# Recurrent-memory attention: the softmax of heads 16 to 31 moved ahead of the queries of heads 0 to 15, and the last tokens projected for sixteen segments at a time

## The chip, the cores and the metric

The kernel runs on one core of a Trainium2 chip (trn2). The time is device time in microseconds (us) of one execution of the whole program, and the median over runs is compared. A profiled execution of the same kernel gives the trace from which all durations below are taken.

## The reference, cut to what matters

The input x has 2048 tokens of width 640 in bf16. Four layers run one after the other, A, B, A, B, each on the layer norm of x and each added to x. Both A layers are the same linear-memory attention and are not touched. A B layer is a segmented attention with a recurrent memory of 8 tokens:

```python
for s in range(n_seg):                       # 64 segments of 32 tokens
    h = concatenate([mem, xs])               # 8 + 32 = 40 tokens
    q, k, v = h @ Wq, h @ Wk, h @ Wv         # 32 heads of width 128
    p = softmax(where(mask, q @ k.T * scale, -1e9))
    o = (p @ v) @ Wo                         # back to width 640
    mem = o[:8]                              # the next segment's memory
    outs.append(o[8:])                       # 32 rows of output
```

The rows of `o` are shifted by 8 against the tokens: the memory that a segment hands on comes from its first 8 rows. So segment s+1 can't be projected before segment s is finished, and the whole B layer is a chain of 64 steps.

## The kernel before

All weights of a B layer lie in SBUF. A step works on 32 columns (`cols_of`): 8 columns of memory that the last step made and 24 columns of the next segment. Projecting those takes the weights as the moving operand: `thin_mm` runs 20 matmuls of 512 columns, four at a time in four strips of 32 columns of the array, and gives the projection of 16 heads for the 32 tokens. There are six such blocks in a step: Ka, Qa, Kb, Qb (keys and queries, a for heads 0 to 15, b for heads 16 to 31) and, later, Va and Vb. The remaining 8 tokens of each segment, here called its last tokens, don't depend on the chain. They are projected ahead of time and kept in DRAM (`QKd` for queries and keys, `VTd` for values), from where every step loads its own share.

The step in its written order, which is also the order of every compute engine's queue (each instruction of TensorE, ScalarE, VectorE and GpSimd is tied to the one written before it on that engine; only the DMA queue of SyncE is ordered by the scheduler):

- The four blocks Ka, Qa, Kb, Qb; each is copied to SBUF (`kq`), transposed (`transp4`, tiles TPak, TPaq, TPbk, TPbq) and scattered into the head-wise tiles `KT` and `QT`: the 8 memory columns by VectorE for this step, the 24 others by ScalarE for the next.
- `mask_mm` writes the mask into the two score tiles in PSUM: SP0 with groups 0 to 7 (the last tokens of all heads, and heads 0 to 15), SP1 with groups 8 to 11 (heads 16 to 31). `scores` adds the products.
- The softmax: `soft_max`, `soft_sub` and `soft_sum` on VectorE, `soft_exp` on ScalarE, then the reciprocal and the products `Px` on VectorE and `Pm` on GpSimd. Meanwhile TensorE does Va, Vb and the first 30 matmuls of `tail_unit`.
- `p_transp` (PTP) transposes the probabilities, `pv` (OTP) multiplies them by the values, `o_mm` (OPS, and OPSd for the deferred rows, `od_chunk`) multiplies by Wo.
- The 8 new memory rows go from OPS by ScalarE (`msb`) to TensorE (MT, which transposes them) and by VectorE (`b_HX`) into the columns of the next step. Between the parts of MT lie the matmuls of `vtail_unit`.

The work on last tokens is cut into units, one for each step. A batch T holds 8 segments, 64 tokens (`TX[T]`), and has eight units. `tail_unit` has 40 matmuls with a 128x128 piece of Wq or Wk as the stationary operand and 64 moving columns; `vtail_unit` has 20 matmuls of 256 moving columns in strips of 32. Steps without a unit of their own repeat one as filler (`work`). A layer norm is made for 128 tokens (`ln_norm`, then `ln_spread`, five transposes), and its result is shared out: 24 tokens of each segment to `HX`, 8 to `TX`.

PSUM is a ring of five shared buffers (`ps_tile`) besides a few of their own (`po`): a tile must be read out before the fifth tile after it can be written.

Of the kernel before, what the change touches and what calls it, by code (L numbers as in the profile page):

```python
# [29 lines left out]
NCH = 5  # L30
# [568 lines left out]
def layer_B(nc, tc, C, W, x_src, xb_src, x_dst, mem0, B_Wv, B_Wo, nsteps=64, out_bf16=False, tag=""):  # L599
# [4 lines left out]
    NT = nsteps // 8  # L604
    QKd = tc.dram_tile([nsteps, 128, 512], BF16, name=f"b_QKd{tag}")
    VTd = tc.dram_tile([nsteps, 8, 4096], BF16, name=f"b_VTd{tag}")
    with ExitStack() as ctx:
# [4 lines left out]
        hp = pool("b_hx", 4)  # L612
# [73 lines left out]
        def ln_load(g, home=None):  # L686
            pool_, tg = home or (bx, "xt")
            xt = pool_.tile([128, D], BF16, name="b_xt", tag=tg)
            nc.sync.dma_start(xt[:], xb_src[128 * g:128 * g + 128, :])
            ln_xt[g] = xt  # L690

        def ln_norm(g):
            xt = ln_xt[g]
            layernorm_tile(nc, sml, C, xt[:], xt[:], "b_ln")
            ln_ready.append(g)

        def ln_spread(g):
            xt = ln_xt.pop(g)
            tps = ps_tile([128, NCH, 4, 32], BF16, "b_lntps")
            for c in range(NCH):  # L700
                nc.tensor.transpose(tps[:, c, :, :].rearrange("p i t -> p (i t)"), xt[:, 128 * c:128 * c + 128], C.identb[:])
            HX[g] = hp.tile([128, NCH, 4, 32], BF16, name="b_HX", tag="HX")
            T, half = divmod(g, 2)
            if half == 0:
                TX[T] = tx.tile([128, NCH, 8, 8], BF16, name="b_TX", tag="TX")
            nc.scalar.copy(HX[g][:, :, :, 8:32], tps[:, :, :, 0:24])
            nc.scalar.copy(TX[T][:, :, 4 * half:4 * half + 4, :], tps[:, :, :, 24:32])
# [6 lines left out]
        def thin_mm(cols_ap, Wt, b, name):  # L714
            ps = ps_tile([128, 512], F32, name)
            for c in range(NCH):
# [38 lines left out]
        tail_ps = {}  # L755

        def tail_unit(T, k, i0, i1, shared=False):
            proj, hg = divmod(k, 4)
            Wt = W.wk if proj else W.wq
            if i0 == 0:  # L760
                if shared:
                    tail_ps[0] = ps_tile([128, 8, 64], F32, "b_tail")
                else:
                    tail_ps[0] = po.tile([128, 8, 64], F32, name="b_tail", tag="tail")
            ps = tail_ps[0]
            for i in range(i0, i1):
                h = 8 * hg + i
                for c in range(NCH):
                    nc.tensor.matmul(ps[:, i, :], lhsT=Wt[:, c, 128 * h:128 * h + 128], rhs=TX[T][:, c, :, :].rearrange("p s t -> p (s t)"),
                                     start=(c == 0), stop=(c == NCH - 1))  # L770

        def tail_evac(T, k, eng, home=None):
            proj, hg = divmod(k, 4)
            pool_, tg = home or (wk, "tu")
            tu = pool_.tile([128, 8, 8, 8], BF16, name="b_tu", tag=tg)
            evac(eng, tu[:].rearrange("p s h t -> p h s t"), tail_ps[0][:].rearrange("p h (s t) -> p h s t", t=8),
                 None if proj else SCB)
            o = 256 * proj + 64 * hg
            nc.sync.dma_start(QKd[8 * T:8 * T + 8, :, o:o + 64].rearrange("s p f -> p s f"), tu[:].rearrange("p s h t -> p s (h t)"))

        def vtail_unit(T, k, c0=0, c1=NCH, ps=None):
            b4, ch = divmod(k, 2)
            if ps is None:
                ps = ps_tile([128, 256], F32, "b_vtail")
            for c in range(c0, c1):
                for q in range(4):
# [6 lines left out]
        def vtail_evac(T, k, ps, eng, home="vt"):  # L793
            b4, ch = divmod(k, 2)
            vt = wk.tile([128, 256], BF16, name="b_vt", tag=home)
            evac(eng, vt[:], ps[:])
            for jj in range(2):
                o = 512 * (2 * b4 + jj) + 256 * ch
                nc.sync.dma_start(VTd[8 * T:8 * T + 8, :, o:o + 256].rearrange("s t f -> (s t) f"), vt[64 * jj:64 * jj + 64, :])
# [17 lines left out]
        n0 = min(4, NG)  # L817
        for g in range(n0):
            ln_load(g, homes[g])
        load_B_wv(nc, W, B_Wv)  # L820
        for g in range(min(2, n0)):
            ln_norm(g)
# [5 lines left out]
        for k in range(8):  # L828
            tail_unit(0, k, 0, 8, shared=True)
            tail_evac(0, k, "act" if k % 2 == 0 else "dve", (kqp, "kq"))  # L830
            if k % 4 == 1 and 2 + k // 4 < n0:
                ln_norm(2 + k // 4)
            if k % 4 == 3 and 2 + k // 4 < n0:
# [24 lines left out]
        if NT > 1:  # L858
            tail_unit(1, 0, 0, 8, shared=True)
            tail_evac(1, 0, "act")  # L860
            vtail_evac(1, 0, vtail_unit(1, 0), "dve")
# [46 lines left out]
        def ln_g(s):  # L908
            return 2 * (s // 8) + 4 + (s % 8 == 5)

        def ln_xt_due(s):
            return s % 8 in (2, 5) and ln_g(s) < NG

        for s in range(nsteps):
# [3 lines left out]
            unit = None  # L918
            if (s + 1) // 8 + 1 < NT:
                unit = ((s + 1) // 8 + 1, (s + 1) % 8)  # L920
            work = unit or (None if last else (NT - 1, 0))
# [24 lines left out]
            def scores(SPs):  # L946
                for b in range(2):
                    for j in range(4):
                        for i in range(4):
                            h = 16 * b + 4 * j + i  # L950
                            nc.tensor.matmul(SPs[b][32 * i:32 * i + 32, j + 4 * (1 - b), :], lhsT=QT[s][:, h, :], rhs=KT[s][:, h, :],
                                             start=False, stop=True, tile_position=(0, 32 * i), skip_group_check=True)
                    if b == 0:
                        qz = QZ[s % 2][:].rearrange("p x c -> p (x c)")
                        for j in range(4):
                            for e in range(2):
                                for t4 in range(4):
                                    pr = 8 * (t4 // 2) + 2 * j + t4 % 2
                                    nc.tensor.matmul(SPs[0][32 * t4:32 * t4 + 16, j, :], lhsT=qz[:, 24 * pr + 8 * e:24 * pr + 8 * e + 16],
                                                     rhs=KT[s][:, 2 * pr + e, :],  # L960
                                                     start=False, stop=True, tile_position=(0, 32 * t4), skip_group_check=True)
# [6 lines left out]
            def soft_max(a, SP):  # L968
                nc.vector.tensor_reduce(out=negmax[:, slice(*GR[a])], in_=SP[:], axis=AX.X, op=ALU.max, negate=True)

            def soft_sub(a, SP):
                n_ = GR[a][1] - GR[a][0]
                nc.vector.tensor_tensor(out=SP[:], in0=SP[:], in1=negmax[:, slice(*GR[a])].unsqueeze(2).to_broadcast([128, n_, 40]), op=ALU.add)

            def soft_exp(a, SP):
                nc.scalar.activation(out=E_[:, slice(*GR[a]), :], in_=SP[:], func=ACT.Exp)

            def soft_sum(a):
                nc.vector.tensor_reduce(out=ssum[:, slice(*GR[a])], in_=E_[:, slice(*GR[a]), :], axis=AX.X, op=ALU.add)
# [24 lines left out]

            Ka = thin_mm(cols, W.wk, 0, "b_Ka")
            ka = kq(Ka, "act")
            Qa = thin_mm(cols, W.wq, 0, "b_Qa")
            qa = kq(Qa, "dve", SCB)
            Kb = thin_mm(cols, W.wk, 1, "b_Kb")
            kb = kq(Kb, "act")  # L1010
            Qb = thin_mm(cols, W.wq, 1, "b_Qb")
            qb = kq(Qb, "act", SCB)

            TPak = transp4(ka, "b_TPak")
            scatter("dve", TPak, 0, KT[s], 0, 8, 32)
            x_scatter(TPak, 0, KT)
# [3 lines left out]
            TPbk = transp4(kb, "b_TPbk")  # L1020
            scatter("dve", TPbk, 1, KT[s], 0, 8, 32)
            x_scatter(TPbk, 1, KT)
            SPa = mask_mm(0)
            TPbq = transp4(qb, "b_TPbq", po.tile([128, 4, 128], BF16, name="b_TPbq", tag="tail"))
            scatter("dve", TPbq, 1, QT[s], 0, 8, 24)
            x_scatter(TPbq, 1, QT)
            SPb = mask_mm(1)
            scores((SPa, SPb))
            soft_max(0, SPa)
            soft_max(1, SPb)  # L1030
            soft_sub(0, SPa)
            soft_exp(0, SPa)
            soft_sub(1, SPb)
            soft_exp(1, SPb)
            soft_sum(0)
            soft_sum(1)
# [14 lines left out]
            if work:  # L1051
                tail_unit(work[0], work[1], 0, 6)
# [7 lines left out]
            if work:  # L1060
                tail_unit(work[0], work[1], 6, 8)
            if unit:
                tail_evac(unit[0], unit[1], "act")
# [22 lines left out]
            if ln_xt_due(s):  # L1086
                ln_norm(ln_g(s))
# [25 lines left out]
            vtail_some(NCH)  # L1113
            if unit:
# [113 lines left out]
```

## Time and profile before

| | |
|---|---|
| median of 3 runs | 2796.26 us (2792.15 to 2801.13) |
| profiled execution | 2787.25 us, its span 2785.5 us |
| TensorE busy | 2574.7 us (92%), 65414 matmuls |
| VectorE / ScalarE / GpSimd busy | 61% / 57% / 26% |
| first B layer: first Ka of step 0 to first Ka of step 63 | 432.6 to 1379.3 us |
| second B layer, the same | 1819.2 to 2764.0 us |

These two stretches of 63 steps are 1892 us of the span. The time of a matmul in the profile is its latency: matmuls overlap, so what a block of them costs is read from the start of one block to the start of the next. A form such as 128*32 says how many rows and columns of the array a matmul uses.

### The profile page before, as it was taken

What the parts mean: (1) busy time and instruction counts of PE and PEld (TensorE: products, weight loads), DVE (VectorE), ACT (ScalarE), POOL (GpSimd) and SP (SyncE); (2) the same over time, 40 slices, a digit from 0 to 9 for tenths busy, and PEclk for the clock granted to TensorE, in tenths of its full rate; (3) what the DMA queues carried; (4) which work ended last, traced back from release to release, by engine and by line L of the source; (5) the groups of instructions that cost most, each with busy time, mean ns of one, the idle gap of its engine ahead of it and who ended that gap; (6) DMA issues with size and microseconds to landing.
All of it is one profiled execution on the core that took longest, in us unless ns stands there. A gap on an engine that the chain in (4) does not pass through costs nothing. (4 is left out here: it accounts for less than half of the span.)

```text
span 2785.5 us, 146956 instructions
## 1 busy us (share of the span) xinstructions
PE 2574.7 (92%) x65414; PEld 1700.1 (61%) x65480; DVE 1686.6 (61%) x4553; ACT 1584.9 (57%) x3708; POOL 715.2 (26%) x1645
## 2 busy tenths in 40 slices
PE   5888879999999999999978888799999999999998
PEld 3555556666666666666645555556666666666665
DVE  6888854555555555555578888445555555555554
ACT  4888854555555555544458888445555455555443
POOL 4666541111111111111146665411111111111110
PEclk9999979999999999999989999899999999999999
DMA  6111162221212212111120111721211121211110
GB/s 239 41 44 40 30 195 69 45 46 41 45 43 45 43 43 45 43 39 30 41 99 28 51 49 37 231 47 39 42 42 40 40 44 40 43 41 38 39 26 20
DMA packets 322300, 156.36 MB, mean 56 GB/s; under 512 B 245760, under 2 KB 310400, under 8 KB 318592
## 3 DMA queue, kind: packets, MB, share of 16 engines
q1 hardware_dynamic: 320224, 136.47, 19.2%
q8 instruction: 512, 8.39, 1.3%
q10 hardware_dynamic: 1440, 10.49, 1.0%
q14 instruction: 124, 1.02, 0.1%
HBM read 95.15 MB, written 51.71 MB: 53 GB/s over the span
## 5 line engine op out<-in xcount | busy, mean ns | idle before, releaser
L101 PEld LDWEIGHTS <-b_HX 128*32 128x32 bf16 x15360 | 430.2, 97 | 341.0 <-issue 14.1
L101 POOL TENSOR_TENSOR b_Pm<-b_E,b_rs 128x96 bf16<-128x96 bf16 x128 | 63.3, 495 | 1443.2 <-ACT b_Vth L101 1094.2
L400 DVE TENSOR_REDUCE a_nm<-a_S 128x2 f32<-128x1024 f32 (+3 forms) x512 | 396.5, 815 | 51.4 <-PE a_T L101 26.6
L442 ACT ACTIVATE a_PT<-a_T 128x1024 bf16<-128x1024 f32 (+1 forms) x384 | 325.4, 889 | 84.9 <-PE a_T L101 50.6
L101 PE MATMUL b_OPS<-b_wo,b_OTsb 128*32 128x320 bf16 x8192 | 308.0, 301 | 10.3 <-issue 8.5
L101 PEld LDWEIGHTS <-b_OTsb 128*32 128x32 bf16 x8192 | 200.5, 97 | 97.0 <-DVE b_OTsb L101 24.1
L101 DVE CAST b_HX<-b_MT 128x8 bf16<-128x8 f32 x372 | 63.7, 172 | 277.5 <-PE b_MT L101 272.2
L444 POOL TENSOR_SCALAR_AFFINE_SELECT a_PT<-a_PT 128x256 bf16<-128x256 bf16 (+1 forms) x384 | 193.5, 520 | 143.2 <-ACT a_PT L442 141.0
L101 ACT CAST b_msb<-b_OPS 128x64 bf16<-128x64 f32 x378 | 69.3, 256 | 237.7 <-PE b_OPS L101 237.7
L101 ACT CAST b_kq<-b_Kb 128x512 bf16<-128x512 f32 x128 | 74.9, 585 | 201.6 <-PE b_Kb L101 201.6
L101 DVE COPY b_KT<-b_TPak 128x128 bf16<-128x128 bf16 x128 | 28.8, 225 | 227.0 <-PE b_TPak L101 227.0
L101 PE MATMUL b_Va<-b_wv,b_HX 128*32 128x512 bf16 x2520 | 160.8, 380 | 0.0
L101 PE MATMUL b_Vb<-b_wv,b_HX 128*32 128x512 bf16 x2520 | 160.1, 379 | 0.0
L101 PEld LDWEIGHTS <-b_kq 128*128 128x128 bf16 x2080 | 116.8, 98 | 68.8 <-ACT b_kq L101 55.6
L101 PE MATMUL b_Ka<-b_wk,b_HX 128*32 128x512 bf16 x2520 | 158.8, 379 | 0.0
L101 DVE TENSOR_SCALAR b_kq<-b_Qa 128x512 bf16<-128x512 f32 x128 | 88.5, 691 | 115.9 <-PE b_Qa L101 112.9
L101 PE MATMUL b_Kb<-b_wk,b_HX 128*32 128x512 bf16 x2520 | 158.6, 379 | 0.0
L101 PE MATMUL b_Qb<-b_wq,b_HX 128*32 128x512 bf16 x2520 | 158.6, 379 | 0.0
L101 PE MATMUL b_Qa<-b_wq,b_HX 128*32 128x512 bf16 x2520 | 158.6, 379 | 0.0
L101 DVE CAST b_OTsb<-b_OTP 128x160 bf16<-128x160 f32 (+1 forms) x384 | 122.3, 374 | 39.6 <-PE b_OTP L101 39.6
L101 PE MATMUL b_vtail<-b_wv,b_TX 128*32 128x256 bf16 x2880 | 137.7, 271 | 6.6 <-issue 3.5
L101 ACT ACTIVATE b_E<-b_SP 128x320 bf16<-128x320 f32 (+1 forms) x256 | 81.1, 368 | 109.0 <-PE b_Va L101 95.3
(195 smaller groups left out, 5764.8 us busy)
## 6 DMA issues: line engine op xcount, KB each, us to landing
b_QKd<-b_tu SPq DMA_DIRECT2D x128, 128.0 KB
b_tl<-b_QKd SPq DMA_DIRECT2D x128, 128.0 KB
b_wv<-in_B_Wv_dram SPq DMA_DIRECT2D x10, 1024.0 KB
b_wo<-in_B_Wo_dram SPq DMA_DIRECT2D x16, 640.0 KB
b_VTd<-b_vt SPq DMA_DIRECT2D x256, 32.0 KB
b_Vth<-b_VTd SPq DMA_DIRECT2D x512, 16.0 KB
b_XO<-xres SPq DMA_DIRECT2D x256, 30.0 KB
b_wk<-in_B_Wk_dram ACTq DMA_DIRECT2D x5, 1024.0 KB
```

The lines of the kernel that those rows point to most:

```text
L101: r = f(*a, **k)
L400: nc.vector.tensor_reduce(out=nm[:, qc, 2 * pr:2 * pr + 2], in_=X[:, :, o:o + w_], axis=AX.X, op=ALU.max, negate=True)
L442: nc.scalar.activation(out=PT[:, :, b:b + width], in_=Y[:, :, 0:width], func=ACT.Exp, scale=SC)
L444: nc.gpsimd.affine_select(out=dv, in_=dv, pattern=[[0, 2], [0, diag], [1, 128]], compare_op=ALU.is_ge, fill=0.0, base=0, channel_multiplie ...
```

## The change

Three things, all in the B layer.

1. The order of a step. Qb, Kb, Ka come first, then the transposes of b, the mask of SP1, two fifths of Qa (8 of 20 matmuls), the scores of heads 16 to 31, and their maximum and subtraction; then the rest of Qa. The scores of the last tokens and of heads 0 to 15 follow after the transposes of a, and their softmax is done in two halves of four groups.
2. The last tokens in batches of sixteen segments (128 tokens) from segment 8 on; the first batch keeps eight. A batch has sixteen units: `tail_unit` has 20 matmuls of 128 columns (four heads), cut at 4, 9 and 16, and so spread over four places of the step; `vtail_unit` has 5 matmuls of 256 columns with all 128 tokens as the stationary operand. The batches begin at segments 0, 8, 24, 40 and 48; the last begins eight segments early, and its first eight are computed and not stored. In the steps 0 to 6 two units are done.
3. The last tokens get a layer norm of their own (`("t", g)`), 128 last tokens at a time, beside that of the whole rows (`("h", g)`). There are 21 of them in a layer in place of 16.

```diff
-        hp = pool("b_hx", 4)
+        hp = pool("b_hx", 3)
...
-            T, half = divmod(g, 2)
-            if half == 0:
-                TX[T] = tx.tile([128, NCH, 8, 8], BF16, name="b_TX", tag="TX")
-            nc.scalar.copy(HX[g][:, :, :, 8:32], tps[:, :, :, 0:24])
-            nc.scalar.copy(TX[T][:, :, 4 * half:4 * half + 4, :], tps[:, :, :, 24:32])
+            if kind == "h":
+                HX[g] = hp.tile([128, NCH, 4, 32], BF16, name="b_HX", tag="HX")
+                nc.scalar.copy(HX[g][:, :, :, 8:32], tps[:, :, :, 0:24])
+            else:
+                TX[g] = tx.tile([128, NCH, 16, 8], BF16, name="b_TX", tag="TX")
+                nc.scalar.copy(TX[g][:].rearrange("p c s t -> p c (s t)"), tps[:].rearrange("p c i t -> p c (i t)"))
...
@@ tail_unit
+            for n_ in range(n0, n1):
+                i, c = divmod(n_, NCH)
+                h = nh * hg + i
+                nc.tensor.matmul(ps[:, i, :], lhsT=Wt[:, c, 128 * h:128 * h + 128], rhs=TX[T][:, c, 0:ns, :].rearrange("p s t -> p (s t)"),
+                                 start=(c == 0), stop=(c == NCH - 1), skip_group_check=True)
...
@@ vtail_unit
+                if T:
+                    nc.tensor.matmul(ps[:], lhsT=TX[T][:, c, :, :].rearrange("p s t -> p (s t)"), rhs=W.wv[:, c, 256 * k:256 * k + 256],
+                                     start=(c == 0), stop=(c == NCH - 1), skip_group_check=True)
+                    continue
...
+        def tail_work(s):
+            j = s + 1
+            if j < 8:
+                return [(1, 2 * j), (1, 2 * j + 1)]
+            b = 2 + (j - 8) // 16
+            return [(b, (j - 8) % 16)] if b < 5 else []
...
+            Qb = thin_mm(cols, W.wq, 1, "b_Qb")
+            qb = kq(Qb, "dve", SCB)
+            Kb = thin_mm(cols, W.wk, 1, "b_Kb")
+            kb = kq(Kb, "act")
             Ka = thin_mm(cols, W.wk, 0, "b_Ka")
             ka = kq(Ka, "act")
-            Qa = thin_mm(cols, W.wq, 0, "b_Qa")
-            qa = kq(Qa, "dve", SCB)
-            Kb = thin_mm(cols, W.wk, 1, "b_Kb")
-            kb = kq(Kb, "act")
-            Qb = thin_mm(cols, W.wq, 1, "b_Qb")
-            qb = kq(Qb, "act", SCB)
...
+            SPb = mask_mm(1)
+            Qa = thin_mm(cols, W.wq, 0, "b_Qa", 0, 2)
+            scores(1, SPb)
+            soft_max(8, 12, SPb[:])
+            soft_sub(8, 12, SPb[:])
+            thin_mm(cols, W.wq, 0, "b_Qa", 2, NCH, Qa)
+            qa = kq(Qa, "act", SCB)
             TPak = transp4(ka, "b_TPak")
             scatter("dve", TPak, 0, KT[s], 0, 8, 32)
+            SPa = mask_mm(0)
+            if work:
+                tp = tail_unit(work[0], work[1], 0, TCUT[0], tail_tile(1, False))
+            soft_exp(8, 12, SPb[:])
             x_scatter(TPak, 0, KT)
             TPaq = transp4(qa, "b_TPaq")
             scatter("dve", TPaq, 0, QT[s], 0, 8, 24)
             x_scatter(TPaq, 0, QT)
...
+            tail_scores(SPa)
+            scores(0, SPa)
+            soft_max(0, 4, SPa[:, 0:4, :])
+            soft_max(4, 8, SPa[:, 4:8, :])
+            soft_sub(0, 4, SPa[:, 0:4, :])
+            soft_exp(0, 4, SPa[:, 0:4, :])
+            soft_sub(4, 8, SPa[:, 4:8, :])
+            soft_exp(4, 8, SPa[:, 4:8, :])
+            soft_sum(8, 12)
+            soft_sum(0, 4)
+            soft_sum(4, 8)
...
-                tail_unit(work[0], work[1], 0, 6)
+                tail_unit(work[0], work[1], TCUT[0], TCUT[1], tp)
...
-                tail_unit(work[0], work[1], 6, 8)
-            if unit:
-                tail_evac(unit[0], unit[1], "act")
+                tail_unit(work[0], work[1], TCUT[1], TCUT[2], tp)
...
             vtail_some(NCH)
+            if work:
+                tail_unit(work[0], work[1], TCUT[2], 20, tp)
             if unit:
+                tail_evac(unit[0], unit[1], tp, "act")
                 vtail_evac(unit[0], unit[1], vps, "act")
+            for T, k in units[1:]:
+                tp = tail_unit(T, k, 0, 20, tail_tile(T, True))
+                vps = vtail_unit(T, k)
+                tail_evac(T, k, tp, "act")
+                vtail_evac(T, k, vps, "act", "msb")
```

## The prediction

> **What bounds the kernel now.** I read the page first, then the time by stage (busy time of each engine in stretches of the span), the matmuls of Ka by tile, and the timeline of one undisturbed step (step 24 of the first B layer). The change touches nothing but the B layers. Page and stretch:
>
> ```profile
> span 2785.5 us, 146956 instructions
> PE 2574.7 (92%) x65414; PEld 1700.1 (61%) x65480; DVE 1686.6 (61%) x4553; ACT 1584.9 (57%) x3708; POOL 715.2 (26%) x1645
> ...
> 433.00:1379.00 946.00, 931.57 (x27314) 615.57 (x27302) 511.33 (x1596) 483.40 (x1268) 117.90 (x328) 1.00 0.19 41
> ```
>
> In the first B layer TensorE is busy 931.57 of 946 us at a granted clock of 1.00; VectorE and ScalarE are busy half the time. So TensorE sets the step, and whatever delays it or lengthens its stream costs time. The first and last starts of Ka (432.6 and 1379.3 us) give (1379.3 - 432.6) / 63 = 15.03 us a step. TensorE in step 24, starts in the first column:
>
> ```profile
> 795.97 1.25 PE L101 MATMUL b_Qb<-b_wq,b_HX 128*32 128x512 bf16 x20
> 797.15 0.40 PE L101 MATMUL b_TPak<-c_identb,b_kq 128*128 128x128 bf16 x4
> 797.39 0.39 PE L101 MATMUL b_TPaq<-c_identb,b_kq 128*128 128x128 bf16 x4
> ...
> 798.22 0.23 PE L101 MATMUL b_SP<-b_mask,c_identb 128*128 128x160 bf16 x1
> 798.38 0.28 PE L101 MATMUL b_SP<-b_KT,b_QT 128*32 128x40 bf16 x16
> ...
> 798.87 1.28 PE L101 MATMUL b_Va<-b_wv,b_HX 128*32 128x512 bf16 x20
> 799.96 1.27 PE L101 MATMUL b_Vb<-b_wv,b_HX 128*32 128x512 bf16 x20
> 801.16 1.05 PE L101 MATMUL b_tail<-b_TX,b_wq 128*128 128x64 bf16 x30
> 802.22 0.24 PE L101 MATMUL b_PTP<-c_identb,b_Px 128*128 128x128 bf16 x2
> ...
> 802.75 0.45 PE L101 MATMUL b_tail<-b_TX,b_wq 128*128 128x64 bf16 x10
> 803.13 0.52 PE L101 MATMUL b_OTP<-b_PTa,b_Vth 32*128 32x40 bf16 x32
> ...
> 806.63 0.39 PE L101 MATMUL b_vtail<-b_wv,b_TX 128*32 128x256 bf16 x8
> ...
> 807.14 0.28 PE L101 MATMUL b_vtail<-b_wv,b_TX 128*32 128x256 bf16 x4
> 807.25 0.21 PE L101 MATMUL b_MT<-b_sel,b_msb 128*32 128x8 bf16 x8
> ...
> 807.41 0.39 PE L101 MATMUL b_Ka<-b_wk,b_HX 128*32 128x512 bf16 x4
> ```
>
> Step 24 starts at 792.74 and ends at 807.41: 14.67 us. Blocks of 20 follow each other by 1.08. Where the form changes there is a **boundary**: Qb to TPak takes 1.18, Vb to the tail 1.20 (Va to Vb 1.09), the 160-column mask to the scores 0.16 (four 128-column transposes take 0.22, 0.056 each, so 160 columns are 0.07), ten tail matmuls to OTP 0.38 (30 of them stream in 0.87, 0.029 each, so ten are 0.29). Each boundary costs 0.09 to 0.11. The softmax as VectorE shows it:
>
> ```profile
> 799.01 0.72 DVE L101 TENSOR_REDUCE b_negmax<-b_SP 128x8 f32<-128x320 f32 x2 [0.36 <-PE b_SP L101]
> ...
> 801.73 0.78 DVE L101 TENSOR_TENSOR b_Px<-b_E,b_rs 128x256 bf16<-128x256 bf16 x2
> ```
>
> SP0 is complete at 798.74, the maximum starts at 799.01 and PTP at 802.22: a chain of 3.48 us, covered almost wholly by Va, Vb and 30 tail matmuls.
>
> **The change, part by part** (times from the step's start; every row is from step 24 unless said).
>
> *Batches of sixteen.* A tail unit was 40 matmuls of 64 columns, 40 x 0.029 = 1.17 us; it becomes 20 of 128, 20 x 0.056 = 1.12. A vtail unit was five rounds of four concurrent matmuls at 0.11, and becomes five matmuls of 256 columns, 2 x 0.056 = 0.11 each. So a unit costs TensorE the same. But there are more units: the last batch repeats eight segments, so a layer has 8 more, seven in steps 0 to 6 and one ahead of the loop. 16 x (1.12 + 0.55) = **27 us**.
>
> *Boundaries.* A step had five (Qb/TPak, mask/scores, Vb/tail, tail/OTP, OTP/OPSd). It gets fifteen: Ka/TPbq, mask/Qa, Qa/TPak, TPaq/scores, Vb/tail, tail/OTP, OTP/OPSd, then, because vtail is now 128*128 between MTs of 128*32, OPSd/vtail, three vtail/MT, three MT/vtail, and tail/Qb.
>
> *Up to the scores.* Qb 0, Kb 1.08, Ka 2.16, TPbq 3.34, TPbk 3.56, mask 3.78, 8 of Qa 3.95, scores of heads 16 to 31 4.38, the rest of Qa 4.50 to 5.15, TPak 5.25, mask 5.47, 4 tail matmuls 5.62 to 5.84. TPaq is a new wait: ScalarE starts the copy of a block 0.28 after it ends (795.97, 796.25) and takes 0.60, so 5.15 + 0.28 + 0.60 = 6.03, TPaq at 6.05, TensorE waits 0.21. Queued behind it are the scores of the last tokens (6.37 to 6.61) and those of heads 0 to 15, which also wait for VectorE's copy of TPaq (0.20 + 0.23 after its end at 6.27): 6.73 to 6.86. Va then starts at 6.86, where it was 6.13.
>
> *The softmax.* The part of heads 16 to 31 leaves the chain, but that of 0 to 15 becomes two halves of 160 elements, and the instruction order of the changed kernel lists a wait on ScalarE before the second subtraction: the exponential of the first half, in the same tile. So the chain goes from engine to engine. Rows of 160 elements take 0.31 (maximum), 0.32 (subtraction), 0.30 (exponential), 0.31 (sum); VectorE to ScalarE takes 0.11, others 0.03. Maxima 7.13 to 7.67, subtraction to 8.02, exponential to 8.43, subtraction to 8.79, exponential to 9.20, sum to 9.54, reciprocal (0.23) to 9.80, Px (0.43) to 10.26, PTP at 10.33. That is 3.47 after the scores: the chain isn't shorter. The cover is: Va, Vb and 5 tail matmuls end at 6.86 + 1.09 + 1.20 + 0.28 = 9.43, and TensorE waits 0.90. PTP moves from 9.48 to 10.33, **+0.85**.
>
> *From PTP to the end.* PTP takes 0.53 as before, to 10.86. Seven tail matmuls and a boundary are 0.49 in place of 0.38, **+0.11**: OTP at 11.35. From OTP to the end of OPSd nothing changes (3.50): 14.85. The end was 0.78 (806.63 to 807.41). Now: boundary and two vtails 0.32, boundary 0.09 (the msb copies are ready before), MTs 0.13, three vtails 0.33, five boundaries 0.48, four tail matmuls 0.22, boundary 0.09: 1.66, **+0.88**. The next Qb starts at 16.51.
>
> *Hidden.* Five more layer norms a layer: their five transposes (0.29) and copies lie in the wait before PTP, VectorE's share under OPS; without that cover 10 x 0.29 = 3 us. SyncE issues fewer DMAs (stores of 16 segments); QKd and VTd are read steps later. Three HX buffers suffice, since one lives four steps. The tail copy moves on ScalarE ahead of the vt copy, which ends near 1.06, and Kb needs that PSUM buffer at 1.08: 0, at most 0.1 a step (13 us).
>
> *Instruction supply.* The mean step is 0.36 longer than step 24, 45 us over 126 steps, with stalls around OPS that the waits put to "issue". A unit has 35 matmuls fewer, so 70 of the step's 868 rows (a weight load and a matmul each) go, while the step gets 12% longer: 18% fewer rows per us. Between 0 and -45; I take 18% of it, -8.
>
> Sum: 126 x (0.85 + 0.11 + 0.88) = 232; 232 + 27 - 8 = **+251 us** on the profiled 2787.25, 3038. The median of the runs lies 9 us above the profiled execution: **3047 us**.
>
> **The rivals.**
>
> A. The new boundaries are free, because the cost belongs to the places where the trace has it and not to vtail and MT, whose waits it would hide in. Then Va starts at 6.77, and the end is bounded by the msb copy (0.52 after OPS): next step at 15.69, +1.02. 128 + 27 - 8 = 147: **2943**. For it: MT does wait for msb today. Against: all five boundaries of the trace cost the same, in both directions. [...]
>
> B. The second subtraction doesn't wait (the first exponential is done sooner than I reckon). Then the halves overlap, PTP comes at 9.80, 0.53 x 126 = 67 less: **2980**. Against: the wait is in the order.
>
> C. Matmuls of 128 columns with weights of their own cost more than 0.056, as in PTP, where eight take 0.53 (0.066). 11 of a unit's 20 are on the path: 126 x 0.11 + 3 = 17 more, 13 with Kb's buffer: **3077**. [...] The transposes of the trace, each with its own load, run at 0.056 and speak against it.
>
> D. Faster: the stalls of instruction supply around OPS vanish, and boundaries and waits disappear in them. Price -45 against +27 for the units: 2796 - 18 = **2778**. It decides only if boundaries and waits cost under 18 / 126 = 0.14 a step, where I reckon 1.84.
>
> **How the numbers follow.** My forecast has 0.63, A 0.14, B 0.10, C 0.09, D 0.04. The range goes from A to beyond C: 2935 to 3095. A difference of 0.3% (8 us) is about what can be measured: faster 0.03, none 0.01 (D only in part), slower 0.96.
>
> **What would show it.** Right: Qb to Qb near 16.5 in steps 7 to 54 and 1.7 more in steps 0 to 6; about 0.1 between MT and vtail each time; TensorE waiting about 0.9 for b_Px before PTP and 0.2 before TPaq; the second subtraction starting after the first exponential's end. Wrong: MT and vtail following by 0.02 (A), PTP within 3.0 of the scores (B), tail matmuls over 0.06 apart (C), a step under 15.1 (D).

## The result: 8.4% slower, and the profile after

The changed kernel takes 3032.47 us (median of 4 runs, 3029.27 to 3034.19) where the kernel before took 2795.41 beside it: ratio 1.0844, 95% interval 1.0824 to 1.0865. The forecast was 3047 us, the range 2935 to 3095. The profiled execution has a span of 3029.4 us, 243.9 more than before. Page and first B layer by stage (columns as before):

```profile
span 3029.4 us, 139233 instructions
PE 2735.0 (90%) x61450; PEld 1660.0 (55%) x61450; DVE 1767.7 (58%) x4989; ACT 1622.2 (54%) x3844; POOL 721.3 (24%) x1655
...
436.00:1497.00 1061.00, 1004.91 (x25316) 593.09 (x25308) 551.77 (x1812) 502.12 (x1338) 120.46 (x332) 1.00 0.17 37
```

TensorE has fewer matmuls (61450 in place of 65414) and yet more busy time, and in the B layer it is busy 1004.91 of 1061 us, where it was 931.57 of 946: 56 us idle in place of 14. The granted clock is 1.00 in both. The first and the last step of the first B layer begin at these times (first start of the first line, first of the second):

```profile
L101 PE MATMUL b_Qb<-b_wq,b_HX x2520: 379/379/390, 435.5 to 2988.1; 128*32 128x512 bf16 x194
...
L101 PE MATMUL b_Qb<-b_wq,b_HXz x40: 379/379/390, 1497.7 to 3004.7; 128*32 128x512 bf16 x40
```

So the 63 steps of the first layer take 1062.2 us (946.7 before); those of the second, from 1943.8 to 3003.8, take 1059.9 (944.0). Of the 243.9 us, 231.4 lie in the loops, the rest ahead of them and behind. Step 24 again, TensorE:

```profile
845.77 1.26 PE L101 MATMUL b_Qb<-b_wq,b_HX 128*32 128x512 bf16 x20
...
851.88 0.40 PE L101 MATMUL b_TPaq<-c_identb,b_kq 128*128 128x128 bf16 x4
...
852.70 1.25 PE L101 MATMUL b_Va<-b_wv,b_HX 128*32 128x512 bf16 x20
...
854.96 0.45 PE L101 MATMUL b_tail<-b_TX,b_wq 128*128 128x128 bf16 x5
856.17 0.24 PE L101 MATMUL b_PTP<-c_identb,b_Px 128*128 128x128 bf16 x2 [0.76 <-DVE b_Px L101]
...
857.19 0.42 PE L101 MATMUL b_OTP<-b_PTa,b_Vth 32*128 32x40 bf16 x32
...
861.09 0.19 PE L101 MATMUL b_MT<-b_sel,b_msb 128*32 128x8 bf16 x4
861.21 0.28 PE L101 MATMUL b_vtail<-b_wv,b_TX 128*128 128x256 bf16 x1
861.43 0.21 PE L101 MATMUL b_MT<-b_sel,b_msb 128*32 128x8 bf16 x8
861.57 0.28 PE L101 MATMUL b_vtail<-b_wv,b_TX 128*128 128x256 bf16 x1
...
862.37 0.40 PE L101 MATMUL b_Qb<-b_wq,b_HX 128*32 128x512 bf16 x4
```

The step takes 16.60 us; the undisturbed one, that most steps hit, 16.52 (14.68 before). The four lines of MT and vtail show the boundaries: a vtail of 256 columns (0.11) is followed by MT after 0.22, and the eight MTs by vtail after 0.14, where 0.06 to 0.07 passed before. The softmax of the same step, VectorE first and then ScalarE:

```profile
853.61 0.33 DVE L101 TENSOR_TENSOR b_SP<-b_SP,b_negmax 128x160 f32<-128x160 f32 x1
854.37 0.33 DVE L101 TENSOR_TENSOR b_SP<-b_SP,b_negmax 128x160 f32<-128x160 f32 x1 [0.43 <-ACT b_E L101]
...
854.03 0.30 ACT L101 ACTIVATE b_E<-b_SP 128x160 bf16<-128x160 f32 x1 [0.99 <-PE b_Va L101]
854.74 0.30 ACT L101 ACTIVATE b_E<-b_SP 128x160 bf16<-128x160 f32 x1 [0.40 <-DVE b_SP L101]
```

Subtraction, exponential, subtraction, exponential: each starts when the one before has ended, as the prediction has it. The largest of TensorE's waits in the first layer, which was 1.0 us in all and came in 4 steps before, now comes in every step:

```profile
PE b_PTP L101 <- DVE b_Px L101: 43.0, 63, 0.8
```

### The profile page after: what moved, and what is told of

Read it like the earlier page. It is cut to its first block, busy times and chain, and to the rows that moved or that the text cites. A ratio compares the mean times of both kernels' runs of the same rounds, so it can differ in the third digit from the quotient of the medians.

```text
span 3029.4 us, 139233 instructions
## 1 busy us (share of the span) xinstructions
PE 2735.0 (90%) x61450; PEld 1660.0 (55%) x61450; DVE 1767.7 (58%) x4989; ACT 1622.2 (54%) x3844; POOL 721.3 (24%) x1655
## 3 DMA queue, kind: packets, MB, share of 16 engines
q14 instruction: 127, 1.04, 0.1%
## 4 chain that ended last, share of the span: by engine, by line
PE 63%; DVE 16%; ACT 13%; issue 4%; DMA 3%; POOL 1%; SPq 0%; ACTq 0%; DVEq 0%; POOLq 0%
PE b_OPS L101 9%; PE b_Qa L101 5%; PE b_Qb L101 5%; ACT a_PT L442 5%; PE b_Kb L101 5%; PE b_Ka L101 5%; PE b_vtail L101 4%; PE b_SP L101 3%; PE b_tail L101 3%; DVE b_ssum L101 3%; PE b_PTP L101 3%; DVE b_SP L101 3%; DVE a_nm L400 3%; PE b_OTP L101 3%; PE b_OPSd L101 3%
## 5 line engine op out<-in xcount | busy, mean ns | idle before, releaser
L101 PEld LDWEIGHTS <-b_HX 128*32 128x32 bf16 x15360 | 364.8, 96 | 344.8 <-issue 10.4
L101 ACT ACTIVATE b_E<-b_SP 128x160 bf16<-128x160 f32 x384 | 115.8, 302 | 179.7 <-PE b_Va L101 123.2
L101 DVE TENSOR_REDUCE b_negmax<-b_SP 128x4 f32<-128x160 f32 x384 | 112.8, 321 | 121.8 <-PE b_SP L101 121.8
L101 PE MATMUL b_vtail<-b_wv,b_TX 128*128 128x256 bf16 (+1 forms) x1040 | 181.4, 294 | 1.0 <-issue 0.8
L101 PE MATMUL b_Qa<-b_wq,b_HX 128*32 128x512 bf16 x2520 | 171.8, 380 | 0.0
L101 DVE TENSOR_TENSOR b_SP<-b_SP,b_negmax 128x160 f32<-128x160 f32 x384 | 127.8, 333 | 73.0 <-ACT b_E L101 55.1
L101 ACT CAST b_OTsb<-b_OTP 128x320 bf16<-128x320 f32 x256 | 96.5, 429 | 111.5 <-PE b_OTP L101 111.5
```

The source lines that it names most:

```text
L101: r = f(*a, **k)
```

## The experiments

Each run stands beside the kernel before on the same chip. The changed kernel, run once more beside the last of them, gave 3024.99 us and 1.0868 (1.0840 to 1.0896), so a difference of 0.3% between chips or runs says nothing of the kernels. "Step" is the undisturbed step of the trace, which most steps hit.

> The changed kernel once more, beside the others of this call on the same chip: 3015 to 3035, ratio 1.080 to 1.090. It says how much of a difference between runs on different chips is the chip's.

**Boundaries at the end: vtail in strips.**

```diff
-  nc.tensor.matmul(ps[:], lhsT=TX[T][:, c, :, :], rhs=W.wv[:, c, 256 * k:256 * k + 256], ...)
+  for q in range(4):
+      nc.tensor.matmul(ps[32 * q:32 * q + 32, :], lhsT=TX[T][:, c, 4 * q:4 * q + 4, :],
+                       rhs=W.wv[:, c, 256 * k:256 * k + 256], tile_position=(0, 32 * q), ...)
```

> The changed kernel with only the matmuls of vtail_unit of the big batches written as four strips of 32 tokens (form 128*32, 20 matmuls) in place of one full-width matmul (128*128, 5 matmuls); same columns streamed, same results. My theory (each change of form costs TensorE about 0.10 us wherever it stands): six of the fifteen boundaries go (vtail and MT have one form again), the end of a step falls by 0.6 us, the step from 16.52 to about 15.9, and the time by 126 x 0.61 = 77 us to about 2955. Rival A (what the end costs is not the form but the msb copies and the four tail matmuls put there): no change, 3024 to 3040.

Measured: 2970.36 us, ratio 1.0676 (1.0658 to 1.0694), step 16.02. The gain is 0.50 a step, not 0.61; rival A is out. The end of a step:

```profile
901.87 0.39 PE L101 MATMUL b_vtail<-b_wv,b_TX 128*32 128x256 bf16 x8
902.15 0.19 PE L101 MATMUL b_MT<-b_sel,b_msb 128*32 128x8 bf16 x4
902.18 0.28 PE L101 MATMUL b_vtail<-b_wv,b_TX 128*32 128x256 bf16 x4
902.31 0.21 PE L101 MATMUL b_MT<-b_sel,b_msb 128*32 128x8 bf16 x8
902.38 0.28 PE L101 MATMUL b_vtail<-b_wv,b_TX 128*32 128x256 bf16 x4
```

MT now follows after 0.28 where two rounds of vtail stream 0.22, much as in the kernel before (0.27): the load of its weights waits for ScalarE's msb (0.16 in the trace), and this takes back 0.06. That leaves about 0.09 for each of the six boundaries. (The strips are also 20 matmuls with a weight load each in place of 5; whether the change of form costs the time or the loading of the new weights across it, no run separates.)

**The second subtraction ahead of the first exponential.**

```diff
  soft_sub(0, 4, SPa[:, 0:4, :])
+ soft_sub(4, 8, SPa[:, 4:8, :])
  soft_exp(0, 4, SPa[:, 0:4, :])
- soft_sub(4, 8, SPa[:, 4:8, :])
```

> The changed kernel with one line moved: the second subtraction of the softmax of heads 0 to 15 is written ahead of the first exponential, so that it no longer waits on ScalarE. My theory (the wait before PTP is the chain subtraction, exponential, subtraction, exponential): PTP comes 0.35 us earlier, the step is 16.17, the time 44 us less, about 2988. Rival (the wait before PTP is set by something else that comes as late, such as GpSimd's product or VectorE's other work): no change, 3024 to 3040.

Measured: 3013.46 us, ratio 1.0835 (1.0819 to 1.0851), step 16.40: 0.12 of the 0.35. The wait on ScalarE went, and another came in its place (step 20, VectorE and ScalarE):

```profile
780.95 0.70 DVE L101 TENSOR_TENSOR b_SP<-b_SP,b_negmax 128x160 f32<-128x160 f32 x2
...
781.75 0.50 ACT L101 ACTIVATE b_E<-b_SP 128x160 bf16<-128x160 f32 x2 [1.35 <-DVE b_SP L101]
```

The two subtractions take 0.70, so they run one after the other, and the first exponential starts 0.10 after the end of both, 0.47 after the end of the first (about 781.28). The two halves are one tile. In both orders a subtraction, which writes it, starts only when the instruction ahead of it on the other half has ended (854.33, then 854.37 in step 24 above), and an exponential only after every subtraction written ahead of it (0.09 and 0.04 after its end there, 0.10 here). Maxima, which only read, overlap by 0.08 (853.19 to 853.27 in step 24 above). In the kernel before, the two subtractions write two tiles, SP0 and SP1: there the second starts at 800.05, before the first ends at 800.14, and the first exponential starts at 800.25, before the second subtraction ends at 800.37.

**The softmax of heads 0 to 15 in one piece.**

```diff
- soft_max(0, 4, ...) ... soft_max(4, 8, ...) ... soft_sub, soft_exp, soft_sub, soft_exp
+ soft_max(0, 8, SPa[:]); soft_sub(0, 8, SPa[:]); soft_exp(0, 8, SPa[:])
```

> The changed kernel with the softmax of heads 0 to 15 in one piece of eight groups (maximum, subtraction, exponential, sum), all else as changed. My theory (the wait before PTP is the chain over the two halves of one tile, where each instruction waits for the one before): PTP comes 0.32 us earlier, 40 us, about 2990, ratio near 1.070. Rival (the halves cost nothing and the wait is set by the later scores alone): no change.

Measured: 2982.70 us, ratio 1.0721 (1.0697 to 1.0744), 42 us under the changed kernel beside it on the same chip; step 16.21. PTP comes 3.28 us after the last scores begin, where it was 3.58 (852.59 to 856.17):

```profile
778.08 0.28 PE L101 MATMUL b_SP<-b_KT,b_QT 128*32 128x40 bf16 x16
...
781.36 0.24 PE L101 MATMUL b_PTP<-c_identb,b_Px 128*128 128x128 bf16 x2 [0.45 <-DVE b_Px L101]
```

So the chain sets the wait before PTP, and cutting it into halves lengthened it by 0.30.

**Four tail matmuls from the end into the wait**: `TCUT = (4, 13, 20)`.

> The changed kernel with the cuts of the tail unit at 4, 13 and 20 in place of 4, 9 and 16: the four matmuls that stood at the end of the step stand in the wait before PTP. My theory (TensorE idles 0.9 us there, and all work at the end of the step is on the path): 4 x 0.056 = 0.22 us a step, 28 us, about 3004. Rival (the end of the step is bounded by the copies of the new memory and not by TensorE's stream): no change, 3024 to 3040.

Measured: 3000.04 us, ratio 1.0786 (1.0766 to 1.0806), step 16.29: 0.23 a step, as forecast. Work at the end is on the path; in the wait it is free.

**The three repairs together.**

> The changed kernel with strips in vtail_unit, the cuts at 4, 13 and 20, and the softmax of heads 0 to 15 in one piece of eight groups. My theory: the boundaries at the end go from eight to none (0.8 us), the tail matmuls there too (0.22), the chain is 0.33 shorter: 1.35 us a step, 170 us, about 2862, still slower than the kernel before by some 65 us: two boundaries, the rest of the wait before PTP, the wait before TPaq and the eight more units. If these repairs hide each other (rival: one wait takes the place of another), 2900 or more.

Measured: 2879.42 us, ratio 1.0346 (1.0328 to 1.0364), step 15.28: 1.24 of the 1.35. That is more than the three gave alone (0.50, 0.30 and 0.23, in all 1.03). The reckoning, which no other run tests: with strips the four tail matmuls are all that changes form at the end, so that moving them takes two boundaries more. The repaired order still loses to the order before.

**The parts alone.** The batches with the step in its old order and with its old softmax (15 wide tail matmuls ahead of PTP, 5 behind), once with full-width vtail and once in strips; and the order with the old batches (`tail_unit` cut at 8, 18, 32 of 40 matmuls).

> The batches alone: sixteen segments a batch, 20 wide tail matmuls (15 ahead of PTP, 5 ahead of OTP), full-width vtail, layer norm of their own, eight more units a layer, but the step in the order of the kernel before, with its softmax. My theory: eight boundaries at the end of a step (OPSd/vtail, vtail/MT, MT/vtail, vtail/Ka), 0.70 us of a step by the changed kernel's rows, 88 us; 27 us for the units; some 15 less of instruction-supply stalls: 100 us slower than before, ratio 1.03 to 1.04. Rival (the batches, their units and stores carry most of the loss and the order little): 170 us or more, ratio over 1.06.

> The batches alone in the order of before, as the run before it, but with vtail in four strips of 32 tokens, so that no boundary is added. My theory: only the eight more units a layer (27 us) are left, less a few us of stalls for 20 matmuls fewer a step: 15 to 27 us slower than before, ratio 1.005 to 1.010. The difference to the run with full-width vtail is the price of eight boundaries a step, 0.70 x 126 = 88 us less what the waits for msb take back, about 75. Rival A (boundaries free): no difference between the two.

> The order alone: the step in the order of the changed kernel with its softmax, but the batches of eight segments of before, their 40 narrow tail matmuls cut at 8, 18 and 32, vtail in strips, no more units. My theory: PTP comes 0.92 us later as in the changed kernel, the 14 matmuls ahead of OTP cost 0.10 more, the 8 at the end with two boundaries 0.43: 1.45 us a step, 183 us, ratio 1.06 to 1.07. So the order carries two thirds of the loss. Rival (the batches carry it): 60 us or less, ratio under 1.025.

Measured: 2882.93 us, ratio 1.0346 (1.0328 to 1.0364), step 15.39; 2804.44 us, 1.0067 (1.0050 to 1.0084), step 14.68; 2948.79 us, 1.0589 (1.0565 to 1.0612), step 16.04. The first two differ in the form of vtail alone: 0.71 a step, which is 0.09 for each of eight boundaries. Of 126 x 0.71 = 89 us, 78 show in the time: the steps with two units and the stalls (they come below) are 11 us longer in strips. With strips the batches cost 18 us: 25 for the doubled units and 8 outside the loops, less 16 of stalls. The order costs 162 us, two thirds of the loss; 183 were expected, as a step grew by 1.36 and not by 1.45. The parts add to 259 us, 22 more than the 237 of the change. A reckoning that no run tests: the order alone has two boundaries at the end (vtail/tail and tail/Qb), while the change has eight there as the batches alone have. So the sum of the parts counts two too many, 126 x 2 x 0.09 = 23 us.

**A version to beat both**: old order, batches of 8, 16, 16, 16 and 8 with vtail in strips, no unit twice, and no filler (`work = unit`); then the same with filler; then the kernel before without filler.

> A version that may beat both: the order of before, batches of 8, 16, 16, 16 and 8 segments with vtail in strips, so that no unit is done twice, and no filler units in the steps that have none. My theory: the step's stream is that of before; 20 matmuls fewer a step take some 5% of the 45 us of instruction-supply stalls; 16 fewer filler steps' worth of tail and vtail matmuls (each up to 0.8 us) 8 to 13 us; five more layer norms a layer cost up to 3: 5 to 20 us faster, ratio 0.993 to 0.998. Rival (fillers cost nothing since the steps wait there anyway, and stalls don't depend on the rows): ratio 1.000 or above.

> The version with batches of 8, 16, 16, 16 and 8 in the order of before, now with filler units in the steps that have none of their own (it ran without them and took 1.0181 of before). My theory after that run: a step without a unit lets TensorE idle 1.0 us before PTP and again later, and in every second one the granted clock falls (0.57 in a stretch of 4 us, OPS 4.03 us in place of 2.36); in the steps 47 to 62 of a layer that is 12 us. With fillers the ratio falls by 24 us to about 1.0095, and what is left is the seven doubled units a layer (25 us) less stalls. Rival (the loss is that of the doubled units and stalls alone): no change, 1.018.

> The kernel before with its filler units left out (steps 55 to 62 of each layer; their results are used nowhere). My theory: the work saved is given back as waits for Px and for msb, and the clock falls in every second step: 5 to 14 us slower, ratio 1.002 to 1.005. Rival (fillers cost TensorE what they stream): 16 x 0.5 us, ratio 0.997.

Measured: 2837.18 us, ratio 1.0181 (1.0160 to 1.0201); 2803.46 us, 1.0073 (1.0053 to 1.0093); 2794.94 us, 1.0043 (1.0029 to 1.0057). The first was a miss: no filler is not cheaper but dearer. The second gained more than the 24 us expected, the third came as expected. Steps without a unit take 14.64 us at best, so the saved work came back as waits, and about every second one takes 16.3 or more. One of these, the stretch of OPS and TensorE's rows:

```profile
1350.90:1354.90 4.00, 4.00 (x76) 2.60 (x72) 0.63 (x2) 0.74 (x2) 0.40 (x1) 0.57 0.18 53
```

```profile
1348.99 0.24 PE L101 MATMUL b_PTP<-c_identb,b_Px 128*128 128x128 bf16 x2 [0.98 <-DVE b_Px L101]
...
1349.88 0.55 PE L101 MATMUL b_OTP<-b_PTa,b_Vth 32*128 32x40 bf16 x32 [0.21 <-ACT b_PTa L101]
...
1350.95 4.03 PE L101 MATMUL b_OPS<-b_wo,b_OTsb 128*32 128x320 bf16 x64
```

TensorE idles ahead of PTP and again ahead of OTP, the granted clock is 0.57 over the 4 us of OPS, and OPS takes 4.03 in place of 2.36. (Why in this step and not in the one before it, the last section says.) No version beat the kernel before. In none of them were the doubled units had for nothing: a batch of sixteen must be finished before its first segment, so its units start eight steps earlier than those of a batch of eight, and steps 0 to 6 have one slot each.

## Why the prediction was right

*Boundaries, ten more at 0.10.* Right. 0.09 each in the two pairs of runs that differ in the form of vtail (0.71 for eight; 0.50 and the 0.06 of msb for six). The two that the new order adds ahead of the scores were not run by themselves.

*Up to the scores.* TPaq was put at 6.05 and came at 6.11 (851.88), Va at 6.86 and came at 6.93.

*The softmax and the wait.* PTP was put at 10.33 and came at 10.40; the cover ended at 9.47 (854.96 + 0.28), a wait of 0.93 where 0.90 was reckoned. The chain over two engines was the reason, as the one-piece run shows. Rival B is out: the second subtraction does wait, and where it was freed of ScalarE the step gained 0.12 and not 0.53, since a subtraction of one half overlapped with nothing on the other half.

*From PTP to the end.* OTP at 11.35, measured 11.42; the next Qb at 16.51, measured 16.60 in this step and 16.52 in the undisturbed one. The term of 1.84 a step is 1.84 (16.52 - 14.68), 232 us over 126 steps. That it fits to the last digit is luck: PTP came 0.07 later than reckoned, and from OTP to OPS, where no change was put, it is 0.95 (857.19 to 858.14) in place of 1.04 (803.13 to 804.17).

*Hidden.* Right for the transposes of the layer norms: in the 30 of the steps 7 to 62 that have them, the stretch from Vb to PTP, in which they lie, is 0.2 us longer in all than in undisturbed steps.

*Units, 27 us.* The term was mis-sized by some 6 us. The steps 0 to 3 take 17.92 and the steps 4 to 6 18.08, 1.40 and 1.56 more than the others (1.67 was put): 21 us for fourteen. Outside the loops it is 12.5 us (243.9 - 231.4) where 3 were put: 2.9 ahead of the first loop, 6.3 between the two and 3.2 behind the second. The sum took no account of the last step of each layer. In the second layer it reaches PTP after 10.40 in place of 9.47, and the clock falls in it (0.57 over 4 us), where it didn't before (2.36):

```profile
3016.14 4.03 PE L101 MATMUL b_OPS<-b_wo,b_OTsb 128*32 128x320 bf16 x64
```

*Instruction supply, -8 us.* Mis-sized: the steps of both loops take 2122.1 us; 126 x 16.52 and the 21 us of the units are 2102, so 20 us of stalls are left, where 1890.7 - 126 x 14.68 = 41 were before. That is -21, in the profile; the changed kernel's other profile has 15 us left. The stalls are 13 to 27 us in all variants with filler in which the batches or the order changed, so it isn't the rows alone. Where they went can be read from the starts of the blocks in the steps 7 to 62. Before, of 38 us, 21 lay between the start of OPS and that of MT, 9 from there to the next step, 5 ahead of Va and 5 between Vb and PTP. Now 17 of 18 us lie between OPS and MT (12 of 12 in the other profile). So where the change has new waits and boundaries the stalls are gone, which is what rival D supposes, and around OPS they fell less. That the one makes the other is not shown, nor that the supply of instructions is what stalls.

The forecast was 15 us high. The units came out 6 us dearer and the stalls 13 us lower than put; the two errors cancel in part, which is luck, and leave 7. The other 8 are the step from the profiled execution to the median, for which 9 were put: it is 1 here (3031.29 to 3032.47).

*Rivals.* A is out by the strips. C: the tail matmuls follow by 0.056 in the change too (seven start within 0.33 of each other, 856.71 to 857.04), so C is out; no run shows what would carry the time beyond C's 3077 to the upper end of the range. D: the stalls did fall, by half, and that was 21 us against 232.

## What to carry to other kernels

On an engine that is busy 98% of a loop, count the changes of tile form before counting columns: replacing twenty narrow matmuls by five wide ones saved nothing in columns here and cost 0.09 us at each of eight boundaries. Work could be moved into a wait for nothing (0.23 us a step), but the softmax cut into halves of one tile was a longer chain, by 0.30, and not a pipelined one. A batch twice as large must be begun half a batch earlier, and the slots that it needed then cost 1.40 to 1.79 us each, where a unit's matmuls were put at 1.67.

## What the runs showed of the hardware that I had not expected

Filler matmuls whose results nobody reads pay for themselves: the kernel before without them is 0.43% slower. From 1255 to 1380 us, without them and with them:

```profile
1255.00:1380.00 125.00, 114.35 (x3029) 69.06 (x3018) 63.65 (x198) 54.54 (x148) 15.07 (x42) 0.95 0.11 27
```

```profile
1255.00:1380.00 125.00, 123.76 (x3689) 81.08 (x3690) 65.32 (x206) 56.47 (x153) 16.29 (x46) 1.00 0.13 29
```

In the versions without filler the clock falls in about every second step, so it isn't the waits by themselves. The step before the one shown above, from 1324.87 to 1339.51, has the same two (0.98 ahead of PTP, 0.20 ahead of OTP) and keeps its clock:

```profile
1334.35 0.24 PE L101 MATMUL b_PTP<-c_identb,b_Px 128*128 128x128 bf16 x2 [0.98 <-DVE b_Px L101]
...
1336.31 2.36 PE L101 MATMUL b_OPS<-b_wo,b_OTsb 128*32 128x320 bf16 x64
```

The trace's record of the granted clock tells the two steps apart. The falls around them last 3.41 us, at a clock of 0.50, and begin nine times 3.41 us from each other (1320.41 and 1351.13). In the profiles of the kernel before and of the changed kernel, too, every stretch of one clock but the last is a multiple of 3.413 us long (58 stretches, 3.413 to 1085.438). The 3.41 us ahead of the fall at 1351.13 hold both waits whole. In the step before, the same grid has an edge at 1334.06, within the wait ahead of PTP, and cuts it in two. How much idle time it takes is my estimate from TensorE's records, with each matmul taken to stream until 0.16 us before its recorded end (one of 512 columns is recorded with 0.379, and a round of four takes 1.08 / 5 = 0.216). In these two profiles the 30 falls came after stretches of the grid in which nothing streamed for 1.93 to 3.41 us; of the 1598 stretches after which the clock stayed at 1.00, none had more than 1.97, and all but 25 had under 1.70. In the profile of the changed kernel no stretch of the loops has more than 1.70, and the clock stays at 1.00 in spite of a wait ahead of PTP in each of the 63 steps of the first layer (0.93 in step 24); the last step of its second layer waits longer ahead of PTP (1.14 in the trace's row for PTP) and again ahead of OTP (0.20), 2.05 in all in one stretch by this estimate, and loses it. Of the 30 stretches ahead of a fall 28 were not idle as a whole: 1.93 to 3.38 of the 3.41 us.
